# Another order of work at the border between two mixture-of-experts layers

## The chip, the core and the metric

The kernel runs as one launch on one of the eight cores of a Trainium2 chip. Its engines are TensorE (PE, matmuls and transposes; PEld is its weight load), VectorE (DVE), ScalarE (ACT), GpSimd (POOL) and SyncE (SP, which issues most DMAs); each runs its own queue of instructions in order. The metric is the device time of an execution in microseconds, the median of several runs.

## What is computed

A linear attention, then a mixture of experts with one expert for each token, then one with two experts for each token, all in float32:

```python
def reference(**kwargs):
    attn_out = _attn_ref(**attn_kwargs)      # state = alpha*state + k v^T; y = q state   (2 x 8 heads, 768 steps, 48)
    x = attn_out.transpose(0, 2, 1, 3).reshape(B * S, H * D)           # 1536 tokens x 384
    x = _moe_ref(x=x, **moe_kwargs)          # top 1 of 8: gate * (relu(x w1[e]) w2[e]), 384 -> 1024 -> 384
    return _moe2_ref(x=x, **moe2_kwargs)     # noisy top 2 of 8: sum of weight * (relu(x w1[e]) w2[e])
```

In the second layer a token's rows go to two experts, and the two weighted results are added in the output.

## The kernel before, in words

After the attention the kernel works through sixteen jobs, `n` = 0 to 15: the eight experts of layer 1, then the eight of layer 2. A job has a hidden product in eight blocks `f` (`hidden(n, f)`, L623, nine matmuls for each: every float32 product is made of three with operands split in two halves) and a second product in eight blocks (`second(n, f)`, L650, nine matmuls each). The weights come as raw tiles from DRAM (`raw(n, i)`, i = 0, 1 for the two halves of w1 at L505, 2, 3 for those of w2 at L508, 768 KB each, issued by SP). They are split into a high part by ACT (L523) and a low part by DVE or POOL (L524), a piece in each block. The rows of the next job are loaded with `load_x` (L566), transposed by PE and split by ACT and DVE (`split_x`, L582 to L587).

The order is written out by hand. Beside its own work a job advances the remains of the job before it, a generator `prev`: for layer 1 `job_route2` (the routing of the expert's results for layer 2, ending in four indirect DMAs that scatter rows into the DRAM store `xs2`, L158), for layer 2 `finish2` (results transposed by row tile at L834, weighted at L802 or L804, and added into `out` by an indirect DMA, L158). `STEPS` says how many steps `prev` takes in each of the sixteen blocks; one step is always taken ahead of the first block.

The change is at `n == E` (job 8), the first expert of layer 2. While it runs, the last job of layer 1 is still being routed. The rows that the last two experts of layer 1 send to expert 0 of layer 2 can't be there in time; they go into 128 rows of their own at `C0`, and are done apart. In block 3 of job 8's second product `load_late` asks SP for them (L841), and the generator `late_tokens` computes them: step 1 transposes them and splits them (L849 to L852), steps 2 and 3 make the hidden rows, nine matmuls of 512 columns each (L861), then the hidden rows are transposed (L874 to L877), and the last step makes the second product (L886) and adds it to `out`. Ahead of that, in block 0, `order` (L475 to L493) ranks the experts by their counts, so that from expert 2 on SP has to read the expert's number into a register before it can load its weights. The string `AFTER` is the order behind job 8's last block: `f` is a step of `finish2(8)`, `l` a step of `late_tokens`, `x` one of the three parts of `split_x` for expert 1.

PSUM banks are taken in turn from three pools: `pm` of two banks, `ph` of three, `py` of three. A tile waits until the one that had its bank before has been read.

Of the kernel before, what the change touches and what calls it, by code (L numbers as in the profile page):

```python
# [7 lines left out]
F32R = mybir.dt.float32r  # L8
# [8 lines left out]
N, DM, E, F = B * S, H * D, 8, 1024  # L17
# [8 lines left out]
CL = 128  # L26
# [29 lines left out]
LX = 9  # L56
SP = 7
WG = 8
STEPS = ("0110311010110000", "1311101110000000", "1021112010100000")
ENGS = ("VGGGGGGGGVVVVVGV", "GGGGGGGGGGGVGGVG")  # L60
XS = ("467", "267", "677")
LATE_F = 3
AFTER = "ffllxxllllxl"
SAFE = 1e-18
LOW1, LOW2, LOW3 = C1 - 128, C2 - 128, C2 - 256

# [1 line left out]
def body(tc, ap, cap, dbg=False, stop=False):  # L68
    nc = tc.nc
    V, A, G, PE = nc.vector, nc.scalar, nc.gpsimd, nc.tensor  # L70
    with ExitStack() as ctx:
# [15 lines left out]
        def hb(shape, dt=F32):  # L87
            return sb(shape, "h", 18, dt)
# [17 lines left out]
        def pm():  # L106
            return ps("pm", 2)
# [72 lines left out]
        ident = iw2[:, 0, :128]  # L180
# [315 lines left out]
        def raw(n, i):  # L496
            if n >= len(jobs):
                return
            layer = jobs[n][0]
            e = expert(n, mybir.EngineType.SP)  # L500
            one = slice(e, e + 1) if place(n) is None else bass.ds(e, 1)
            w1, w2 = ap[f"w1_{layer}"][one], ap[f"w2_{layer}"][one]
            if i < 2:
                t = s6([128, ND, 512])
                nc.sync.dma_start(t, w1.rearrange("o (d p) f -> p (o d) f", p=128)[:, :, i * 512:(i + 1) * 512])  # L505
            else:
                t = s6([128, 4, DM])
                nc.sync.dma_start(t, w2.rearrange("o (f p) d -> p (o f) d", p=128)[:, (i - 2) * 4:(i - 1) * 4, :])  # L508
            raws[n, i] = t
# [25 lines left out]
        def w2_of(n, f):  # L535
            hi, lo = parts[n, 2 + f // 4]
            return hi[:, f % 4, :], lo[:, f % 4, :]
# [19 lines left out]
        def load_x(n, eng):  # L557
            layer, e = jobs[n]
            nt_, p, c = dims(n)
            store = (xs1, xs2)[layer - 1]  # L560
            g = sb([p, nt_, RW], "b6", 5)
            if place(n) is None:
                rows_ = store[e * R:e * R + nt_ * p]
            else:
                rows_ = store[bass.ds(expert(n, eng.engine) * R, nt_ * p), :]
            eng.dma_start(g, rows_.rearrange("(t p) d -> p t d", p=p))  # L566
            xg[n] = g
            xsp[n] = (xb([128, ND, c], F32R), xb([128, ND, c], F32R))
# [275 lines left out]
        def late_tokens(n, g):  # L844

            xh, xl = xb([128, ND, CL], F32R), xb([128, ND, CL], F32R)
            xp = pm()
            for d in range(ND):
                PE.transpose(xp[:, d * CL:(d + 1) * CL], g[:, 0, d * 128:(d + 1) * 128], ident[:CL, :CL])  # L849
            m = lambda x: x.rearrange("p d c -> p (d c)")  # L850
            A.activation(m(xh), xp[:, :ND * CL], AF.Copy)
            V.tensor_tensor(m(xl), xp[:, :ND * CL], m(xh).bitcast(F32), op=ALU.subtract)  # L852
            yield
            hq = []
            for i in range(2):
                wh, wl = parts[n, i]
                p = ph()[:CL]
                for k in range(3 * ND):
                    d = k // 3
                    x, w = ((xh, wh), (xh, wl), (xl, wh))[k % 3]  # L860
                    PE.matmul(p, x[:, d, :], w[:, d, :], start=(k == 0), stop=(k == 3 * ND - 1))  # L861
                for q in range(2):
                    h = hb([CL, 256])
                    if q:
                        V.tensor_scalar(h, p[:, q * 256:q * 256 + 256], 0.0, None, op0=ALU.max)
                    else:
                        A.activation(h, p[:, :256], AF.Relu)
                    hq.append(h)
                yield
            ht = []  # L870
            for i in range(4):
                tp = pm()[:, :2 * CL]
                for k in range(2):
                    PE.transpose(tp[:, k * CL:(k + 1) * CL], hq[i][:, k * 128:k * 128 + 128], ident[:CL, :CL])  # L874
                hh, hl = hb([128, 2 * CL], F32R), hb([128, 2 * CL], F32R)
                A.activation(hh, tp, AF.Copy)
                V.tensor_tensor(hl, tp, hh.bitcast(F32), op=ALU.subtract)  # L877
                ht.append((hh, hl))
                if i % 2:
                    yield  # L880
            y = py()[:CL, :DM]
            for f in range(NF):
                (hh, hl), (wh, wl) = ht[f // 2], w2_of(n, f)
                sl = slice(f % 2 * CL, f % 2 * CL + CL)
                for k, (l, r) in enumerate(((hh, wh), (hh, wl), (hl, wh))):
                    PE.matmul(y, l[:, sl], r, start=(f == 0 and k == 0), stop=(f == NF - 1 and k == 2))  # L886
            ysc = hb([CL, 1, DM])
            weigh(g[:, :, NZ:NZ + 1], 0, y, tokens_of(g), ysc, [])
            yield
# [215 lines left out]
        for n, (layer, e) in enumerate(jobs):  # L1105
            steps = STEPS[0 if n < E else 1 if n == E else 2]
            eng = [G if x == "G" else V for x in ENGS[layer - 1]]
            step(prev)
            for f in range(NF):
                hidden(n, f)  # L1110
                split_rest()
                step(prev, int(steps[f]))
                if f == (3 if n == E - 1 else 0) and n not in (E, 2 * E - 1):
                    load_x(n + 1, nc.gpsimd)
                if f == 4 and layer == 2:
                    own_weight(n)
                if f % 4 == 2:
                    raw(n + 1, 2 + f // 4)
                if n != E + 1:
                    split(n + 1, f, eng[f])  # L1120
                else:
                    split(n, 8 + f, eng[f])
                    if f >= 4:
                        split_rest()
                        split(n + 1, f - 4, eng[f])
            if n < 2 * E - 1:
                for f in range(NF):
                    if n == E and f == LATE_F:
                        for _ in prev:
                            pass  # L1130
                        g = load_late(nc.sync)
                        load_x(n + 1, nc.sync)
                        it = late_tokens(n, g)
                    xs_ = XS[2 if n == 0 else layer - 1]
                    if n != E and str(f) in xs_:
                        split_x(n + 1, xs_.index(str(f)))
                    second(n, f, by_row(n))
                    split_rest()
                    step(prev, int(steps[8 + f]))
                    if n == E and f == 0:  # L1140
                        order(2, acc2)
                    if f % 4 == 2:
                        raw(n + 2, f // 4)
                    if n < 4 and f == 5:
                        zero_out(n)
                    if n != E:
                        split(n + 1, 8 + f, eng[8 + f])
                    if n == E + 1 and f < 4:
                        split_rest()
                        split(n + 1, 4 + f, eng[8 + f])  # L1150
                if n == E - NL:

                    cp = pm()
                    PE.matmul(cp[:, 0:1], ones, acc2[:, 0:1], start=True, stop=True)
                    V.tensor_scalar(eb3[:, 0:1], cp[:, 0:1], -1.0, float(C0), op0=ALU.mult, op1=ALU.add)
                    V.tensor_scalar(eb3[:, 0:1], eb3[:, 0:1], 0.0, None, op0=ALU.max)
                prev = job_route2(n) if layer == 1 else finish2(n)
                d = 0
                for o in AFTER if n == E else ():
                    if o == "x":  # L1160
                        split_x(n + 1, d)
                        d += 1
                    else:
                        step(prev if o == "f" else it)
            else:
                nt_, p, c = dims(n)
                ix = tokens_of(xg[n])
                ysc = sb([p, nt_, DM], "b6", 5)
                group = []
                it = beyond()  # L1170
                for t in range(nt_):
                    if t:
                        step(it)
                    for f in range(NF):
                        second(n, f, (t,))
                    weigh(own[n], t, yps[n][t][:tiles(n)[t][2], :DM], ix, ysc, group)
# [216 lines left out]
```

## Time and profile before

| | |
|---|---|
| runs, median (lowest to highest) | 500.62 us (499.69 to 501.07) |
| the profiled execution | 503.19 us, span 501.4 us |
| mean granted TensorE clock | 0.985 |
| PE busy | 478.2 us (95%), 3539 instructions |
| PEld busy | 448.2 us (89%) |
| DVE busy | 310.1 us (62%) |
| ACT busy | 262.0 us (52%) |
| POOL busy | 316.5 us (63%) |
| chain that ended last | PE 73%, DVE 14%, issue 4%, ACT 4%, DMA 2% |

The profile is of one execution; its times are counted from the start of its span. In the page's 40 slices of 12.5 us PE is at 9 tenths or more nearly throughout. Near the middle stands one slice at 7, the one from 275.8 to 288.3, and there alone the granted clock is below 9 tenths ahead of the last slice. This is where job 8 ends and job 9 begins: job 8's second product runs from 263.5 to 273.9, and the first hidden block of job 9 starts at 291.4. An engine's idle time costs nothing unless PE waits for it.

### The profile page before, as it was taken

The page shows a single profiled execution, that of the slowest core. Times are in us where ns is not written, and L with a number is a line of the kernel's source. Part 1 is how long each engine was busy: PE and PEld are TensorE (multiplying, and loading weights), DVE is VectorE, ACT ScalarE, POOL GpSimd, SP SyncE. Part 2 cuts the span into 40 slices and gives each one's busy share as a digit, 9 for nine tenths or more (in the row PEclk, how much of TensorE's full clock was granted, in tenths as well). Part 3 has the DMA queues.
Part 4 walks back from the last instruction along what each step waited for, and adds up shares of the span by engine and source line. Part 5 has one row for each costly group of instructions (what it writes and reads, how often), then busy time and mean ns, then how long its engine had stood idle before and what let it go on. Part 6 is the DMA issues. An engine that isn't in the chain of part 4 may idle for free.

```text
span 501.4 us, 9823 instructions
## 1 busy us (share of the span) xinstructions
PE 478.2 (95%) x3539; PEld 448.2 (89%) x3542; DVE 310.1 (62%) x866; ACT 262.0 (52%) x682; POOL 316.5 (63%) x396
## 2 busy tenths in 40 slices
PE   8997999899999999999999799999999999999993
PEld 4586887799999999999988699899999999999993
DVE  8999956656786786776863323925545373655540
ACT  3475686366675676675661248353554535364410
POOL 3444674374876786785864149697594958779322
PEclk9999998999999999999999899999999999999997
DMA  8974663497888777676734644393564927372132
GB/s 287 406 246 160 242 221 127 164 295 233 282 288 249 261 241 241 202 244 203 239 100 130 204 92 132 99 245 106 156 176 129 221 81 203 83 191 25 17 47 43
DMA packets 47798, 91.67 MB, mean 183 GB/s; under 512 B 4624, under 2 KB 29153, under 8 KB 47738
## 3 DMA queue, kind: packets, MB, share of 16 engines
q1 hardware_dynamic: 38090, 70.32, 42.9%
q0 software_dynamic: 9648, 20.61, 17.4%
q8 instruction: 30, 0.49, 0.4%
q14 instruction: 30, 0.25, 0.2%
HBM read 70.63 MB, written 20.28 MB: 181 GB/s over the span
## 4 chain that ended last, share of the span: by engine, by line
PE 73%; DVE 14%; issue 4%; ACT 4%; DMA 2%; POOL 1%; SPq 0%; POOLq 0%; DVEq 0%; ACTq 0%
PE py L650 28%; PE ph L623 27%; DVE s L524 2%; PE pm L582 2%; PE ph L290 2%; DVE h L627 2%; PE pm L366 2%; DVE s L237 2%; PE pm L834 1%; PE py L337 1%; PE pm L678 1%; PE py L343 1%; PE ph L861 1%; ACT s L523 1%; PE py L317 1%
## 5 line engine op out<-in xcount | busy, mean ns | idle before, releaser
L524 POOL TENSOR_TENSOR s<-s,s 128x384 fp32r<-128x384 f32 x175 | 184.8, 1301 | 51.0 <-ACT s L523 45.9
L623 PE MATMUL ph<-x,s 128*128 128x240 f32 (+6 forms) x1152 | 179.9, 311 | 3.1 <-DVE h L627 1.4
L623 PEld LDWEIGHTS ph<-x,s 128*128 128x128 f32 x1152 | 167.6, 189 | 6.9 <-DVE h L627 3.0
L650 PE MATMUL py<-h,s 128*128 128x240 f32 (+5 forms) x1008 | 154.1, 307 | 0.0
L650 PEld LDWEIGHTS py<-h,s 128*128 128x128 f32 x1008 | 142.5, 189 | 1.0
L523 ACT ACTIVATE s<-s 128x384 fp32r<-128x384 f32 x256 | 123.1, 516 | 0.0
L627 DVE SCALAR_TENSOR_TENSOR h<-ph,h 128x240 fp32r<-128x240 f32 (+6 forms) x128 | 61.0, 483 | 67.4 <-ACT h L626 62.0
L524 DVE TENSOR_TENSOR s<-s,s 128x384 fp32r<-128x384 f32 x81 | 89.8, 1128 | 5.6 <-ACT s L523 5.5
L626 ACT ACTIVATE h<-ph 128x240 fp32r<-128x240 f32 (+6 forms) x128 | 55.3, 432 | 62.8 <-PE ph L623 53.5
L158 POOL DMA_INDIRECT out<-b,m_ix x29 | 46.5, 1605 | 45.5 <-ACT b L802 21.0
L586 ACT ACTIVATE x<-pm 128x480 fp32r<-128x480 f32 (+7 forms) x38 | 18.5, 489 | 63.9 <-PE pm L582 63.5
L299 POOL TENSOR_SCALAR_AFFINE_SELECT h<-h 128x512 f32<-128x512 f32 x24 | 22.6, 964 | 39.2 <-ACT h L298 39.2
L158 POOL DMA_INDIRECT xs<-b,m_si x32 | 32.9, 1028 | 15.8 <-DVE pm L759 10.5
L587 DVE TENSOR_TENSOR x<-pm,x 128x480 fp32r<-128x480 f32 (+7 forms) x38 | 20.7, 550 | 31.8 <-ACT x L586 31.5
L650 PE MATMUL py<-s,h 128*128 128x384 f32 x144 | 26.6, 340 | 0.0
L650 PEld LDWEIGHTS py<-s,h 128*128 128x128 f32 x144 | 25.0, 188 | 0.0
L237 DVE TENSOR_TENSOR s<-s,s 112x256 f32<-112x256 f32 (+2 forms) x24 | 19.0, 813 | 0.8 <-DMA s<-qs 0.2
L158 POOL DMA_INDIRECT xs<-s,m_si x12 | 13.1, 1088 | 9.8 <-DVE m_g L405 4.6
L156 POOL MEMSET spacer<- 1x1 f32 x74 | 18.8, 253 | 0.1
L582 PE MATMUL pm<-iw,b 108*128 108x108 f32 (+5 forms) x129 | 18.5, 259 | 0.2 <-DVE accs L760 0.2
L170 PE MATMUL ph<-warm 128*128 128x512 bf16 x63 | 16.2, 410 | 1.7 <-POOL warm L165 1.5
L797 DVE TENSOR_REDUCE m_own<-m_ox 108x4 f32<-108x24 f32 (+1 forms) x6 | 1.1, 176 | 24.6 <-POOL m_ox L795 23.5
(234 smaller groups left out, 544.9 us busy)
## 6 DMA issues: line engine op xcount, KB each, us to landing
s<-w SPq DMA_DIRECT2D x64, 768.0 KB, 5.4
xs<-s SPq DMA_DIRECT2D x2, 1576.0 KB, 6.4
out<-s SPq DMA_DIRECT2D x4, 768.0 KB, 7.8
b<-xs POOLq DMA_DIRECT2D x4, 664.9 KB
b<-xs POOLq DMA_DIRECT2D x7, 369.4 KB
s<-as SPq DMA_DIRECT2D x2, 780.5 KB
s<-ks SPq DMA_DIRECT2D x2, 768.0 KB, 9.5
s<-qs SPq DMA_DIRECT2D x2, 768.0 KB
```

The source lines that it names most:

```text
L156: G.memset(spacer, 0.0)
L158: st = G.indirect_dma_start(out=dst, out_offset=bass.IndirectOffsetOnAxis(ap=ix, axis=0), in_=src, in_offset=None, **kw)
L237: eng.tensor_tensor(o, src[:, h].rearrange("r (s j) -> r s j", j=64), x[:, h].rearrange("r (s j) -> r s j", j=64), op=ALU.mult)
L299: G.affine_select(a_, a_, pattern=[[0, 4], [1, 128]], compare_op=ALU.is_ge, fill=0.0, base=0, channel_multiplier=-1)
L523: A.activation(hi[sl], t[sl], AF.Copy)
L524: rest.append(lambda: (eng or V).tensor_tensor(lo[sl], t[sl], hi[sl].bitcast(F32), op=ALU.subtract))
L582: PE.transpose(xp[:, k * c + sl.start:k * c + sl.stop], g[:r, t, d * 128:(d + 1) * 128], ident[:r, :r])
L587: V.tensor_tensor(m(xl), xp[:, :w], m(xh).bitcast(F32), op=ALU.subtract)
L623: PE.matmul(p, w, x[:, d, :], start=(k == 0), stop=(k == 3 * ND - 1))
L626: A.activation(hh, p, AF.Relu)
L627: V.scalar_tensor_tensor(hl, p, 0.0, hh.bitcast(F32), op0=ALU.max, op1=ALU.subtract)
L650: PE.matmul(out_, l, r, start=(f == 0 and k == 0), stop=(f == NF - 1 and k == 2))
```

## The change

Four things are altered. `STEPS` for job 8: the step that computes the row weights is taken in hidden block 5 and no longer in 6, and the rank matmul and the scatters follow together in hidden block 7, where the scatters before came in block 0 of the second product. The order behind job 8 (`AFTER`): the late rows are transposed ahead of row tile 0, row tile 1 comes ahead of the late products, and the transposes of the hidden rows alternate with those of expert 1's rows. The hidden rows of the late tokens are transposed four to a bank instead of two, the second four in a bank of `ph`, and evicted with half as many instructions of double width. And the load of the first half of w1 for job 10 stands on SP's queue behind the late rows' load and that of expert 1's rows, and no longer a block ahead of them.

```diff
-STEPS = ("0110311010110000", "1311101110000000", "1021112010100000")
+STEPS = ("0110311010110000", "1311110200000000", "1021112010100000")
-AFTER = "ffllxxllllxl"
+AFTER = "flfflllxlxxl"
@@ late_tokens
             ht = []
-            for i in range(4):
-                tp = pm()[:, :2 * CL]
-                for k in range(2):
-                    PE.transpose(tp[:, k * CL:(k + 1) * CL], hq[i][:, k * 128:k * 128 + 128], ident[:CL, :CL])
-                hh, hl = hb([128, 2 * CL], F32R), hb([128, 2 * CL], F32R)
+            for i in range(2):
+                tp = (pm, ph)[i]()[:, :4 * CL]
+                for k in range(4):
+                    PE.transpose(tp[:, k * CL:(k + 1) * CL], hq[2 * i + k // 2][:, k % 2 * 128:k % 2 * 128 + 128],
+                                 ident[:CL, :CL])
+                hh, hl = hb([128, 4 * CL], F32R), hb([128, 4 * CL], F32R)
                 A.activation(hh, tp, AF.Copy)
                 V.tensor_tensor(hl, tp, hh.bitcast(F32), op=ALU.subtract)
                 ht.append((hh, hl))
-                if i % 2:
-                    yield
+                yield
             y = py()[:CL, :DM]
             for f in range(NF):
-                (hh, hl), (wh, wl) = ht[f // 2], w2_of(n, f)
-                sl = slice(f % 2 * CL, f % 2 * CL + CL)
+                (hh, hl), (wh, wl) = ht[f // 4], w2_of(n, f)
+                sl = slice(f % 4 * CL, f % 4 * CL + CL)
@@ the second product's blocks
                         g = load_late(nc.sync)
                         load_x(n + 1, nc.sync)
+                        raw(n + 2, 0)
                         it = late_tokens(n, g)
...
-                    if f % 4 == 2:
+                    if f % 4 == 2 and (n, f) != (E, 2):
                         raw(n + 2, f // 4)
```

## Rows read from the trace of the kernel before

**Rows 1.** Chain of waits, 261 to 306: start, length, engine, tile, line, count.

```profile
265.19 8.42 PE py L650 x60
...
274.40 2.46 DMA h<-xs
...
278.03 3.84 PE ph L861 x9
...
282.61 2.12 PE ph L861 x9
...
291.31 0.33 PE pm L834 x3
...
293.75 12.37 PE ph L623 x63
```

**Rows 2.** Timeline of PE: start, length, instruction, idle before and releaser.

```profile
263.25 0.17 PE L743 MATMUL pm<-accs,tri 120*120 120x8 bf16 x1 [0.47 <-DVE m_wt L738]
...
276.90 0.55 PE L849 MATMUL pm<-iw,h 128*128 128x128 f32 x3 [2.06 <-DMA h<-xs]
...
285.98 0.77 PE L874 MATMUL pm<-iw,h 128*128 128x128 f32 x4 [0.83 <-DVE h L877]
...
323.25 1.25 PE L623 MATMUL ph<-x,s 128*128 128x432 f32 x5 [1.07 <-DVE x L587]
```

**Rows 3.** Timeline of SP's queue: end of layer 1, and the border.

```profile
100.17 0.37 SPq L606 DMA_DIRECT2D b<-xs  x1
...
268.47 0.00 SPq L505 DMA_DIRECT2D s<-w  x1
274.40 0.34 SPq L841 DMA_DIRECT2D h<-xs  x1
```

**Rows 4.** Waits of SP's queue, 240 to 345: total, times, longest.

```profile
SPq L841 <- DMA xs<-b,m_si: 5.9, 1, 5.9
```

**Rows 5.** Timeline of POOL: the last scatter of layer 1, and the border.

```profile
97.47 0.98 POOL L158 DMA_INDIRECT xs<-s,m_si  x1 [1.85 <-DVE acc L441]
...
257.95 6.84 POOL L524 TENSOR_TENSOR s<-s,s 128x384 fp32r<-128x384 f32 x7 [2.39 <-ACT s L523]
...
264.99 1.00 POOL L158 DMA_INDIRECT xs<-b,m_si  x1 [0.18 <-DVE accs L760]
...
268.89 0.99 POOL L158 DMA_INDIRECT xs<-b,m_si  x1 [0.22 <-issue]
...
291.84 1.61 POOL L158 DMA_INDIRECT out<-h,m_ix  x1 [14.43 <-ACT h L802]
...
296.96 1.60 POOL L158 DMA_INDIRECT out<-b,m_ix  x1 [3.47 <-DVE h L627]
...
300.78 21.00 POOL L524 TENSOR_TENSOR s<-s,s 128x384 fp32r<-128x384 f32 x21
```

**Rows 6.** Windows: PE, PEld, DVE, ACT, POOL busy; PEclk; DMA share; GB/s.

```profile
81.80:83.10 1.30, 0.06 (x2) 0.03 (x1) 0.68 (x2) 1.30 (x5) 0.00 (x0) 1.00 0.20 62
83.40:86.40 3.00, 3.00 (x16) 2.91 (x14) 2.00 (x8) 2.34 (x7) 1.25 (x3) 0.50 0.57 152
...
268.50:270.50 2.00, 2.00 (x16) 2.00 (x16) 0.00 (x0) 0.00 (x0) 1.24 (x4) 1.00 0.67 60
270.50:274.00 3.50, 3.50 (x27) 3.34 (x25) 0.37 (x1) 0.42 (x1) 0.00 (x0) 1.00 0.81 309
...
278.00:281.00 3.00, 2.97 (x7) 2.40 (x8) 0.56 (x1) 0.00 (x0) 0.00 (x0) 0.50 0.93 286
```

**Rows 7.** Timeline of ACT and DVE: the late rows' copies, one subtraction, a split.

```profile
277.48 0.49 ACT L851 ACTIVATE x<-pm 128x384 fp32r<-128x384 f32 x1 [2.02 <-PE pm L849]
278.00 0.56 DVE L852 TENSOR_TENSOR x<-pm,x 128x384 fp32r<-128x384 f32 x1 [3.23 <-ACT x L851]
...
311.91 10.30 DVE L524 TENSOR_TENSOR s<-s,s 128x384 fp32r<-128x384 f32 x1 [0.69 <-ACT s L523]
...
320.07 0.52 ACT L523 ACTIVATE s<-s 128x384 fp32r<-128x384 f32 x1
```

## The prediction

> **What bounds the kernel now.** I read the page first: TensorE (PE) is busy 95% of the span, no other engine above 63%, so only what stands on PE's way can move the end. The 40 slices show one place in the middle where PE falls to 7 and its clock to 8: the border between the two layers. Then I read the chain of waits there [rows 1], PE's own idle times [rows 2], and what SP and POOL were doing [rows 3 to 5]. The reader is to see this. PE works without a gap from 265.19 for 8.42 us, to 273.61, on expert 0's second product. It then transposes row tile 0 and stands for 2.06 us, until the late rows arrive [rows 2]. They were asked for at 274.40, since SP stood 5.9 us at that load for the scatters that write those rows [rows 3, 4]. The first product on the late rows then runs at half speed: nine matmuls take 3.84 us, the next nine 2.12 [rows 1], and the granted clock is 0.50, the 1.2 GHz level [rows 6]. A last gap of 0.83 us follows at the transposes of the late hidden rows [rows 2]. Far behind, at 323.25, PE waits 1.07 us for a piece of x of expert 2 [rows 2].
>
> The sum is made in the profiled execution: 501.4 us of span, 503.19 us in all. The median of the runs is 500.62, 2.57 lower; I take the difference in time over to the median unchanged.
>
> **The change, part by part.** Times at which nothing is said of a source are those of the step before plus the named duration.
>
> Row weights a block ahead. In the trace PE waits 0.47 us at L743 for the row weights' product (DVE L738) [rows 2], though the rank matmul doesn't use it; it shares its PSUM bank. One hidden block earlier that product is done before PE asks. The 0.47 us is not won: the next thing PE needs is the count in the matmul of `order` (L475), whose operand DVE writes last of all (L760, just before the first scatter [rows 5]). PE reaches that matmul earlier and waits there. DVE's chain itself only moves by the order of a tenth, since its last links hang on the last hidden block's eviction. Cost and gain: 0 (bounds: 0.47 gained, 0.2 lost by a later sixth eviction, which nobody waits for).
>
> The scatters. They are now emitted ahead of the last of the seven POOL subtractions (6.84 us for seven [rows 5], 0.98 each). POOL is free 0.98 us earlier, but the row numbers come from DVE, so the first scatter can gain between 0 and 0.98; I take 0.25, since DVE's L760 ended only 0.18 us before it started. The last then ends its issue at 268.89 + 0.99 - 0.25 = 269.63.
>
> The weight load behind the late rows' load. This is the largest term. Before, SP issued 768 KB of weights at 268.47, in the middle of the four scatters, and was released by the scatters at 274.40, that is 4.52 us after the last scatter's issue ended [rows 3, 5]. The weight load is in flight for just this time: from 268.5 to 270.5 the transfers move 60 GB/s with the engines two thirds busy, and only then does the rate rise [rows 6]. The nearest row without such a neighbour is the last scatter of layer 1: issued at 97.47 for 0.98 us, SP released at 100.17, 1.72 us after [rows 3, 5]. So the landing takes between 1.72 and 4.52 us; I take 1.72, for the same kind of transfer with nothing beside it. SP then issues the late rows' load at 271.35, and at 2.46 us [rows 1] plus 0.04 they are there at 273.85. Upper end: 274.15 and 276.65.
>
> A page speaks against this. The Trainium skill, "DMA: Bandwidth & Descriptors", section "Anatomy of one DMA — SWDGE (gpsimd) path", puts about 2.0 us of a transfer down to a fixed cost, mostly the receipt of the last write, heaviest for DRAM; no removal of traffic shortens that. With about half a microsecond of data it would make some 2.5 us (an estimate from that page) where the row has 1.72, and the sum some 0.8 us smaller; 1.72 measured here already includes such a receipt, so the row decides.
>
> What the moved weight load costs: SP's register load, the load of expert 1's rows and then the weights follow at about 272.5 instead of 268.47. The weights are split first in the fourth block of expert 1's hidden layer, near 300; a load of that size lands in single microseconds. Cost 0. Behind the waiting late load on SP stand expert 1's rows and two weight loads; the rows go out about 3 us earlier than before, so nobody waits longer for them.
>
> Late transposes ahead of the row tiles. PE finishes the second product at 273.61 and finds the late rows at 273.85: a wait of 0.24 us in place of 2.06. Row tile 0 moves behind them, into the time in which ACT and DVE copy the transposed rows (ACT starts 0.58 us after PE, 0.49; DVE ends 1.66 us after PE's start [rows 2, 7]). But tile 1 is now third in a pool of two banks and waits for DVE's copy: to 273.85 + 1.66 = 275.51. With its 0.33 us [rows 1] the first late product starts at 275.85; before it was 278.03. Gain 2.18.
>
> From there to the second hidden block of expert 1 the trace has 293.75 - 278.03 = 15.72 us [rows 1]. Off this go: 3.84 - 2.12 = 1.72, if the clock stays at its upper level, because the wait before is 0.24 + 0.8 and not 2.06; the 0.83 us gap, now filled by a group of expert 1's transposes; and 0.33 for tile 1, already counted. Rest 12.84.
>
> Four to a bank. Eight transposes stay eight; four pairs of evictions become two pairs of double width. Nothing at 512 columns of this kind stands in the trace: between the 384-column rows of 0.49 (ACT) and 0.56 (DVE) [rows 7] and a third more, 0.65 and 0.75. The new order puts the second and third x groups behind these copies on DVE, each in a bank that must be free; I work out waits on PE of about 0.5 and 0.25 us. So plus 0.75 (0 to 1.6). 12.84 + 0.75 = 13.59, and the second hidden block starts at 275.85 + 13.59 = 289.44. Border gain: 293.75 - 289.44 = 4.31 us.
>
> The wait at 323. One DVE subtraction, two operands in SBUF, took 10.30 us from 311.91 [rows 7], until POOL's run of 21 subtractions, 21.00 us from 300.78 [rows 5], was over; the split of x behind it made PE wait 1.07 us. POOL started that run late: tile 1's scatter stood from 293.5 to 296.96 behind the late rows' scatter of 291.84, then came tile 2's and a load [rows 5]. With tile 1's scatter moved ahead of the late one, one step of 1.91 us falls out. Against PE's second hidden block, the run began 300.78 - 293.75 = 7.03 us after it. Now the late product ends 2.11 us before that block (2.44 from tile 1 to it [rows 1], less one tile), its scatter follows 0.9 later, the run 8.94 - 1.91 = 7.03 us after that: 5.82. POOL is 1.21 us ahead and through with twenty of the 21 at 319.57 on the old scale; the operand of the last comes at 320.59 [rows 7], so POOL pauses a microsecond and DVE gets through: 1.07 us gained. It needs a lead of more than 0.2 us. The Trainium skill, "SBUF — State Buffer", section "SBUF: two separate sides", says that a DVE instruction with two SBUF inputs and a GpSimd one exclude each other for a whole instruction; by that rule alone DVE would wait for one subtraction, about 1 us, and the wait at 323 would not hang on POOL's start. The row has 10.30, so the trace decides.
>
> Sum: 4.31 + 1.07 = 5.38. The profiled execution would take 503.19 - 5.38 = 497.8, the median 500.62 - 5.38 = 495.24, so 495.2.
>
> **The rivals.**
> (a) The clock falls again: PE's small waits (0.24, then 0.8 with a few transposes between) are enough. For it: a wait of 1.24 us (1.30 with 0.06 of work) was followed by 0.50 from 83.40 on [rows 6]. Against: the 1.07 us at 322 had no such effect (the page's clock row stays at 9). Price 1.72: 3.66 gained, 497.0.
> (b) The wait at 323 stays, because POOL's lead is eaten on its way: 4.31, 496.3. With (a) as well: 2.6, 498.0.
> (c) The scatters land no faster without the weight load, at 276.65 the late rows come as before, and PE, which can no longer do tile 0 first, stands 3 us. The first late product starts at 276.65 + 1.66 + 0.33 = 278.64, at half speed: 278.64 + 13.59 + 1.72 = 293.95, 0.2 later than before, against 1.07 won: 499.8. For it: the four scatters are 480 separate rows and not 128. Against: their bytes flow at POOL's pace until the weights come in.
> (d) Slower: as (c), but PE stays at the low level through both late products and into the third. A low stretch costs half its length. Without it (c) would gain 293.75 - 292.23 + 1.07 = 2.59, so it decides from 5.2 us at the low level; the stretches in the trace lasted a little over 3 us [rows 6]. Three of them at 3.3, 9.9 us, cost 4.95 and give 500.62 + 2.36 = 503.0.
>
> **How the numbers follow.** Forecast 0.46, with its own range of 494.4 to 496.4 (the two bounds of the x waits and 0.7 us of landing); (a) 0.16; (b) 0.14; (a) with (b) 0.05; (c) 0.15; (d) 0.04. About 0.3%, 1.5 us, is what a measurement can tell. Faster: the first four and a little of (c), 0.82; same 0.13; slower 0.05. The range runs from 494.0 to 499.0: it takes in (a), (b) and both, leaves out (c) and (d).
>
> **What would show it.** The late load's issue near 271.4 and under 2 us behind the last scatter; no weight load in flight then; PE's wait at L849 under 0.5 us, a new one of about 0.8 at L834, none of 0.83 at L874; both groups of nine at L861 near 2.1 us; the clock row without the 8; a new wait of about 0.4 at L475; two evictions of 128x512; tile 1's scatter ahead of the late one; no DVE subtraction of 10 us and no wait of 1.07 at L623. The prediction is wrong if the late load is still issued near 274, or if L861's first nine still take 3.8.

## The result and the profile after

The changed kernel takes 494.86 us, median of four runs (494.43 to 495.22), where the kernel before took 500.53 beside it (499.69 to 501.07): a ratio of 0.9888, 95% interval 0.9871 to 0.9905, so 5.67 us less. 495.2 was forecast. The later groups of runs were on chips on which the kernel before takes between 501.5 and 505.0 us, so there only ratios are compared.

The two profiled executions differ by 8.8 us, more than the medians. Job 8 already starts 2.47 us earlier (247.81 against 250.28), ahead of anything that was changed. Another 0.69 us lies in job 8's hidden blocks, where the execution before has a wait of 0.56 us for DVE. That wait comes and goes whatever the kernel: the changed kernel's second profile has it (0.57), and before_fill, with the old `STEPS`, has it not. So I compare distances between three marks on PE that lie behind it: R, the long run of job 8's second product behind `order`; H, the first hidden block of expert 1; K, expert 2's hidden blocks behind its first row tile. PE's timeline of the kernel before (start, length, instruction) has them here:

```profile
265.05 8.96 PE L650 MATMUL py<-h,s 128*128 128x304 f32 x63
...
291.40 2.02 PE L623 MATMUL ph<-x,s 128*128 128x432 f32 x9
...
293.50 12.61 PE L623 MATMUL ph<-x,s 128*128 128x432 f32 x63
...
321.23 0.95 PE L623 MATMUL ph<-x,s 128*128 128x432 f32 x4
...
324.34 0.83 PE L834 MATMUL pm<-iw,b 128*108 128x128 f32 x3
324.93 3.79 PE L623 MATMUL ph<-x,s 128*128 128x432 f32 x18
```

And PE's timeline of the changed kernel, with the idle time before an instruction and its releaser in brackets:

```profile
261.85 0.18 PE L475 MATMUL pm<-accs,ones 128*128 128x8 bf16 x1 [0.58 <-DVE accs L760]
261.89 8.97 PE L650 MATMUL py<-h,s 128*128 128x304 f32 x63
271.03 0.52 PE L849 MATMUL pm<-iw,h 128*128 128x128 f32 x3 [0.17 <-DMA h<-xs]
...
272.60 0.54 PE L834 MATMUL pm<-iw,b 128*108 128x128 f32 x3 [0.73 <-ACT b L802]
272.89 4.41 PE L861 MATMUL ph<-s,x 128*128 128x512 f32 x18
277.13 0.60 PE L874 MATMUL pm<-iw,h 128*128 128x128 f32 x4
...
279.15 1.10 PE L582 MATMUL pm<-iw,b 108*128 108x108 f32 x8 [0.48 <-DVE h L878]
...
284.29 0.49 PE L834 MATMUL pm<-iw,b 128*88 128x128 f32 x3
284.54 14.39 PE L623 MATMUL ph<-x,s 128*128 128x432 f32 x72
...
314.05 1.94 PE L623 MATMUL ph<-x,s 128*128 128x432 f32 x9
315.83 0.49 PE L834 MATMUL pm<-iw,b 128*108 128x128 f32 x3
316.07 3.79 PE L623 MATMUL ph<-x,s 128*128 128x432 f32 x18
```

R to H was 26.35 and is 22.65; H to K was 33.53 and is 31.53; together 59.88 and 54.18, that is 5.70 less, as much as the 5.67 of the medians. The reader is to see four things. The wait for the late rows is 0.17 us and no longer 2.06 [rows 2]. All eighteen matmuls on the late rows take 4.41 us, where the first nine alone took 3.84 [rows 1]. The 0.83 ahead of L874 has gone, and three waits are new: 0.58 at L475, 0.73 at row tile 1, 0.48 at the x groups. And nothing waits at 314, where 1.07 stood [rows 2].

SP's queue shows why the late rows are there:

```profile
268.51 0.34 SPq L841 DMA_DIRECT2D h<-xs  x1
269.07 0.33 SPq L566 DMA_DIRECT2D b<-xs  x1
270.27 1.13 SPq L505 DMA_DIRECT2D s<-w  x2
```

And POOL's timeline shows the last scatter, then the late rows' scatter, tile 2's, and the run of subtractions:

```profile
265.55 0.98 POOL L158 DMA_INDIRECT xs<-b,m_si  x1 [0.22 <-issue]
...
285.40 1.59 POOL L158 DMA_INDIRECT out<-h,m_ix  x1 [8.95 <-ACT h L802]
290.46 1.60 POOL L158 DMA_INDIRECT out<-b,m_ix  x1 [3.43 <-DVE h L627]
...
293.00 19.50 POOL L524 TENSOR_TENSOR s<-s,s 128x384 fp32r<-128x384 f32 x20
313.48 1.01 POOL L524 TENSOR_TENSOR s<-s,s 128x384 fp32r<-128x384 f32 x1 [0.97 <-ACT s L523]
```

The late load goes out 268.51 - 266.53 = 1.98 us behind the end of the last scatter's issue, where it was 4.52 [rows 3, 5]. The DMA queues show what was in the way. POOL's scatters go through the queue q0, SP's loads through q1; each row has packets, MB, and share of the 16 DMA engines. This is all that moved in the kernel before from 268.90 to 271.50, that is 3.85 to 6.45 us behind R, with the scatters still to land:

```profile
q1 hardware_dynamic: 192, 0.39, 81.5%
```

And in the changed kernel the same distance behind R, from 265.74 to 268.34:

```profile
q0 software_dynamic: 128, 0.38, 53.1%
```

While the weights come in, the scatters' queue stands still for 2.6 us, about the 2.54 by which they land later (4.52 - 1.98). Why it stands still no run here shows.

POOL's run has a pause of 0.97 us ahead of its last subtraction, and there DVE gets through; on DVE's timeline the two subtractions end at 313.40, ahead of PE's need:

```profile
278.40 0.69 DVE L878 TENSOR_TENSOR h<-pm,h 128x512 fp32r<-128x512 f32 x1 [0.23 <-ACT h L877]
...
304.73 8.67 DVE L524 TENSOR_TENSOR s<-s,s 128x384 fp32r<-128x384 f32 x2 [0.69 <-POOL s L524]
```

### The profile page after: what moved, and what is told of

Same layout as the page of the kernel before. It is cut to its first block, busy times and chain, and to the rows that moved or that the text cites. A ratio compares the mean times of both kernels' runs of the same rounds, so it can differ in the third digit from the quotient of the medians.

```text
span 492.7 us, 9819 instructions
## 1 busy us (share of the span) xinstructions
PE 475.2 (96%) x3539; PEld 446.8 (91%) x3542; DVE 315.1 (64%) x864; ACT 262.0 (53%) x680; POOL 315.8 (64%) x396
## 4 chain that ended last, share of the span: by engine, by line
PE 80%; DVE 11%; ACT 3%; issue 3%; DMA 2%; POOL 1%; SPq 0%; POOLq 0%; DVEq 0%
PE py L650 31%; PE ph L623 30%; PE pm L582 3%; PE ph L290 2%; PE pm L366 2%; PE py L337 2%; DVE s L237 2%; PE pm L834 2%; DVE h L627 1%; DVE s L524 1%; PE py L343 1%; PE pm L678 1%; PE py L317 1%; PE py L284 1%; DVE s L254 1%
## 5 line engine op out<-in xcount | busy, mean ns | idle before, releaser
L524 DVE TENSOR_TENSOR s<-s,s 128x384 fp32r<-128x384 f32 x81 | 95.2, 1195 | 4.4 <-ACT s L523 3.6
L299 POOL TENSOR_SCALAR_AFFINE_SELECT h<-h 128x512 f32<-128x512 f32 x24 | 21.6, 921 | 39.4 <-ACT h L298 39.4
```

The lines of the kernel that those rows point to most:

```text
L299: G.affine_select(a_, a_, pattern=[[0, 4], [1, 128]], compare_op=ALU.is_ge, fill=0.0, base=0, channel_multiplier=-1)
L524: rest.append(lambda: (eng or V).tensor_tensor(lo[sl], t[sl], hi[sl].bitcast(F32), op=ALU.subtract))
```

## The experiments

The theory: the weight load beside the scatters delayed their landing, the wait for the late rows let the clock fall, and the new order starts POOL's run early enough for DVE. The rival: the order of work carries the gain, and the load was hidden anyway. The marks of all kernels, each from one profiled execution, in us:

| kernel | R to H | H to K | sum | ratio to before, 95% interval |
|---|---|---|---|---|
| before | 26.35 | 33.53 | 59.88 | |
| changed | 22.65 | 31.53 | 54.18 | 0.9888 (0.9871 to 0.9905) |
| changed, second group | 22.70 | 31.54 | 54.24 | 0.9865 (0.9836 to 0.9895) |
| changed, third group | 22.74 | 31.53 | 54.27 | 0.9863 (0.9835 to 0.9892) |
| load_only | 22.85 | 33.38 | 56.23 | 0.9910 (0.9877 to 0.9943) |
| no_load_move | 26.70 | 31.53 | 58.23 | 0.9971 (0.9939 to 1.0004) |
| no_steps | 22.98 | 31.53 | 54.51 | 0.9878 (0.9814 to 0.9942) |
| decoy | 29.33 | 31.53 | 60.86 | 1.0017 (0.9988 to 1.0047) |
| before_fill | 25.13 | 33.52 | 58.65 | 0.9974 (0.9949 to 1.0000) |
| tile1_late | 22.25 | 33.99 | 56.24 | 0.9927 (0.9898 to 0.9955) |
| two_to_bank | 26.05 | 31.50 | 57.55 | 0.9940 (0.9914 to 0.9966) |
| tile1_between | 22.44 | 31.53 | 53.97 | 0.9876 (0.9846 to 0.9907) |
| tile1_between_ph | 22.55 | 31.53 | 54.08 | 0.9864 (0.9835 to 0.9892) |
| best | 22.64 | 31.42 | 54.06 | 0.9850 (0.9823 to 0.9878) |

Where row tile 2 comes behind expert 1's first block (before, load_only, before_fill, tile1_late), it takes 0.33 us of H to K (two blocks start 2.10 us apart with it between them, 1.77 without); elsewhere it takes 0.25 of R to H (284.54 - 284.29). The three profiles of the changed kernel agree within 0.09 us. The runs alone set load_only apart from the kernel before; the intervals of no_load_move, before_fill and decoy reach 1, so what is said of these three rests on the traces.

**load_only**: one edit on the kernel before.

```diff
                         load_x(n + 1, nc.sync)
+                        raw(n + 2, 0)
...
-                    if f % 4 == 2:
+                    if f % 4 == 2 and (n, f) != (E, 2):
```

> The kernel before with the weight load of expert 2 moved behind the late rows' load, and nothing else. Theory (traffic and clock): without the load beside them the scatters land about 2 us after the last issue instead of 4.5, the late load goes out 2.5 us earlier, PE's wait at the late transposes shrinks from 2.06 to under 0.5 us, and with it the half-speed stretch of the first late product goes (1.7 us). The gap of 0.83 at the hidden rows' transposes and the wait at 323 stay. About 3.7 us faster, 496.8. Rival (the order of work is what counts, the load is hidden anyway): less than 1.5 us, 499 or more.

PE's timeline, with SP and POOL under it:

```profile
276.80 0.49 PE L849 MATMUL pm<-iw,h 128*128 128x128 f32 x3
278.01 2.48 PE L861 MATMUL ph<-s,x 128*128 128x512 f32 x9 [0.72 <-ACT x L851]
...
321.70 1.24 PE L623 MATMUL ph<-x,s 128*128 128x432 f32 x5 [0.89 <-DVE x L587]
```

```profile
273.95 0.34 SPq L841 DMA_DIRECT2D h<-xs  x1
```

```profile
270.97 0.98 POOL L158 DMA_INDIRECT xs<-b,m_si  x1 [0.21 <-issue]
```

3.65 us less between the marks, where 3.7 were expected; the landing is 273.95 - 271.95 = 2.00 us, PE doesn't wait at L849, and the wait far behind stays. The first nine matmuls take 2.48 us for 3.84, which is 1.36 of the 1.7 expected there. This edit alone is two thirds of the gain; the rival falls.

**no_load_move**: the changed kernel without that edit.

> The changed kernel with the weight load back at its old place ahead of the late load; row weights, order and banks as changed. Theory: the scatters land 4.5 us after their issue again, the late rows come near 276.5 on the old scale, PE stands some 3 us and the first late product runs at 1.2 GHz; only the wait at 323 and the gap of 0.83 are won: 498.3 to 499.7. Rival (order counts, load is hidden): within 0.7 us of the changed kernel, 495.5.

PE's timeline, SP's queue, and windows (PE, PEld, DVE, ACT, POOL busy; PEclk; DMA share; GB/s):

```profile
277.48 0.52 PE L849 MATMUL pm<-iw,h 128*128 128x128 f32 x3 [2.91 <-DMA h<-xs]
...
279.59 5.48 PE L861 MATMUL ph<-s,x 128*128 128x512 f32 x18
```

```profile
274.88 0.34 SPq L841 DMA_DIRECT2D h<-xs  x1
```

```profile
278.00:282.00 4.00, 3.28 (x12) 2.55 (x11) 1.18 (x2) 0.96 (x2) 2.44 (x3) 0.57 0.98 323
```

The late load goes out 4.62 us behind the last scatter's issue (270.26), PE stands 2.91 us, the clock falls to 0.57, and R to H is even 0.35 longer than before. The border is then about what rival (c) of the prediction has (0.2 later), though (c) has the scatters land late without the weight load too, and load_only shows that they don't. The 1.65 us that are left come from behind H, where 2.00 are won.

**decoy**: a copy at the old place, for nobody.

```diff
+        decoy = dram.tile([DM, F], F32, name="decoy")
...
+                    if (n, f) == (E, 2):
+                        nc.sync.dma_start(decoy, ap["w1_2"][bass.ds(expert(n + 2, mybir.EngineType.SP), 1)].rearrange("o d f -> (o d) f"))
```

> The changed kernel with one DMA more: the same 768 KB of expert 2's weights copied from DRAM to a DRAM scratch, issued by SP where the weight load stood before; nobody reads it. Theory (bytes in flight delay the scatters): the landing goes back from 2.0 to 4 us or more, the late load goes out 2 to 3 us later, PE's wait at the late transposes is 2 to 3 us, the clock falls behind it: 498 to 500. Rival (it is not the bytes but what the weight load did to buffers or to SP's order): as the changed kernel, 494.9 within 0.5.

From the copy's buffer on this kernel's line numbers are higher by one, so L842 here is L841 in the others. SP's queue, its issue of the copy with the size, POOL's last scatter, and PE:

```profile
276.60 0.35 SPq L842 DMA_DIRECT2D h<-xs  x1
```

```profile
decoy<-w SPq DMA_DIRECT2D x1, 1536.0 KB
```

```profile
269.60 0.99 POOL L159 DMA_INDIRECT xs<-b,m_si  x1 [0.22 <-issue]
```

```profile
279.16 0.87 PE L850 MATMUL pm<-iw,h 128*128 128x128 f32 x3 [4.28 <-DMA h<-xs]
```

The last scatter's issue ended at 270.59, so the landing took 6.01 us, and PE stood 4.28. The copy was to be of the weight load's size, but it takes all of expert 2's w1, 1536 KB where the load has 768, and it writes them to DRAM too. 498 to 500 was expected, and the marks put it 0.98 us above the kernel before, so I had its price about 1.5 us or more too low. So it is no measure of the weight load's own price. What it shows is that a transfer that nobody reads, and that has none of the weight load's buffers, delays the scatters as well: from 271.05 to 274.75 only q1 has packets. It stands on SP's queue where the load stood, so by itself it doesn't rule out SP's order; but in both kernels SP did nothing behind that issue but wait for the scatters (5.9 us [rows 4] and 7.2).

**before_fill**: the kernel before, with useless matmuls in the wait.

```diff
-AFTER = "ffllxxllllxl"
+AFTER = "ffwllxxllllxl"
...
+                    elif o == "w":
+                        warm(9)
```

> The kernel before with nine matmuls of 128x512 on a constant tile put on PE between row tile 0 and the late rows' transposes, nothing else: work that nobody uses, in the wait of 2.06 us. Theory (the wait lets the granted clock fall, and that is what the first late product pays): the clock stays at 2.4 GHz, the first nine matmuls take 2.1 to 2.5 us and not 3.84, the late rows come as before: 1.2 to 1.8 us faster than the kernel before. Rival (the product is slow because of the transfers beside it, or its operands come late): 3.8 us still, no difference.

```profile
272.03 1.89 PE L170 MATMUL ph<-warm 128*128 128x512 bf16 x8
274.10 0.55 PE L849 MATMUL pm<-iw,h 128*128 128x128 f32 x3 [0.18 <-DMA h<-xs]
275.23 2.48 PE L861 MATMUL ph<-s,x 128*128 128x512 f32 x9 [0.58 <-ACT x L851]
```

```profile
276.00:278.00 2.00, 2.00 (x11) 1.48 (x12) 0.00 (x0) 0.26 (x1) 0.00 (x0) 1.00 0.86 291
```

Eight of the nine are recorded. The late rows come no earlier (their transposes start 11.92 us behind R, before 11.85), yet the first nine matmuls take 2.48 us at a granted clock of 1.00, with 291 GB/s of transfers beside them: 1.23 us less in all. The wait set the clock, not the transfers.

**no_steps**: the old `STEPS` string in the changed kernel.

> The changed kernel with the old STEPS string (row weights and scatters a block later). Theory: the wait of 0.47 at the rank matmul comes back, the new wait of 0.58 at the matmul of the counts goes, the scatters start 0.3 us later, and PE waits 0.3 us more for the late rows: 0 to 0.5 us slower than the changed kernel, 494.9 to 495.4. Rival (the earlier scatters carry the gain): 1.5 us or more slower, 496.4 and up.

Behind R it is 0.24 to 0.33 us longer; PE waits 0.50 for the late rows. Ahead of R the 0.47 and the 0.58 trade places: from PE's readiness for the rank matmul to R it is 262.78 to 265.05, 2.27 us, before [rows 2], and 259.51 to 261.89, 2.38 us, changed. From job 8's start to R the old string takes 14.77 to 14.79 us in the profiles that have the wait of 0.56 for DVE, and the new one 14.71 to 14.76. The runs can't tell this from nothing.

**tile1_late**: row tile 1 goes back into expert 1's job.

```diff
-AFTER = "flfflllxlxxl"
+AFTER = "flflllxlxxl"
```

> The changed kernel with row tile 1 not ahead of the late products but in expert 1's job, as before (one step fewer behind job 8). Theory (POOL's lead ends the wait far behind): PE has no wait of 0.73 for tile 1's bank and starts the late product 0.7 us earlier, but tile 1's scatter stands behind the late one again, POOL's run of subtractions starts 1.9 us later, the DVE subtraction takes 10 us again and PE loses 1.1 us at expert 2's first hidden block and about 0.6 at the row tile behind it: 0.5 to 1.3 us slower than the changed kernel. Rival (the wait at 323 went for another reason, such as the earlier border): 0.7 us faster than the changed kernel.

```profile
319.13 1.25 PE L623 MATMUL ph<-x,s 128*128 128x432 f32 x5 [1.55 <-DVE x L587]
```

```profile
296.66 21.00 POOL L524 TENSOR_TENSOR s<-s,s 128x384 fp32r<-128x384 f32 x21
```

POOL's run has no pause again and PE waits 1.55 us. The direction was right, the size was not: 2.0 us slower than the changed kernel between the marks, not 0.5 to 1.3. PE gained 0.4 at the border and not 0.7, and 0.25 of it is only tile 2, now behind H; there 2.46 were lost, 0.33 of them by tile 2. POOL's run starts 7.74 us behind expert 1's second block (296.66 - 288.92), later than in the kernel before (300.78 - 293.50 = 7.28), and so the wait is longer than 1.07.

**two_to_bank**: the changed kernel with the four banks of two from before (the lines that follow from this are left out).

```diff
-            for i in range(2):
-                tp = (pm, ph)[i]()[:, :4 * CL]
+            for i in range(4):
+                tp = pm()[:, :2 * CL]
```

> The changed kernel with the hidden transposes two to a bank again, all in the pool of two. Theory: with the x groups between them the two banks turn over more often, each turn waiting for a copy on ACT and DVE: 0.5 to 1.5 us more between the late product and expert 1's first block. Rival (the width of the evictions doesn't matter, or shorter ones free the banks sooner): within 0.3 us of the changed kernel, or faster.

```profile
278.06 0.59 PE L582 MATMUL pm<-iw,b 108*128 108x108 f32 x4 [0.82 <-DVE h L877]
...
281.96 5.41 PE L886 MATMUL py<-s,h 128*128 128x384 f32 x24
```

```profile
277.00:279.00 2.00, 1.05 (x9) 0.57 (x7) 1.09 (x3) 1.08 (x4) 0.00 (x0) 1.00 1.10 322
279.00:281.00 2.00, 0.94 (x6) 0.59 (x6) 1.13 (x3) 0.99 (x4) 0.00 (x0) 0.92 1.07 284
281.00:283.00 2.00, 1.71 (x7) 1.71 (x8) 0.97 (x3) 0.96 (x2) 0.00 (x0) 0.50 0.43 146
```

3.3 us more, where I expected 0.5 to 1.5. PE is busy half of the time from 277 to 281 in short waits for copies, and then the clock falls as it did behind a long wait; the late rows' second product takes 5.41 us for 4.43. I had left that out.

**tile1_between**, **tile1_between_ph**, **best**: attempts to take the new waits away.

```diff
-AFTER = "flfflllxlxxl"
+AFTER = "flflfllxlxxl"        # tile1_between, tile1_between_ph
+AFTER = "flflfllxlfxxl"       # best
...
-                tp = (pm, ph)[i]()[:, :4 * CL]
+                tp = ph()[:, :4 * CL]        # tile1_between_ph, best
```

> The changed kernel with row tile 1 between the two late products (order f l f l f l l x l x x l). Theory: its bank is free by then, so the wait of 0.73 on PE goes, and its scatter is still ahead of the late one: 0.5 to 0.8 us faster than the changed kernel. Rival (the wait only moves to the expert's transposes, whose banks hang on the same DVE copies): within 0.2 us of it.

> The kernel with tile 1 between the late products, and both banks of hidden transposes taken from the pool of three. Theory: the wait of 0.48 at the second x group goes, since its bank no longer hangs on the copy of the first four; the third group still waits for DVE, some 0.25 us: 0.2 to 0.5 us faster than with tile 1 between alone. Rival (DVE's copies are the bound, whatever the bank): within 0.1 us of it.

> Tile 1 between the late products, both banks of hidden transposes from the pool of three, and row tile 2 also behind job 8, ahead of the second x group (order f l f l f l l x l f x x l). Theory: tile 2's transposes fill half of the wait of 0.62 at the x groups, tile 1's wait of 0.73 stays away, and POOL, which no longer has to wait for the late scatter's landing, starts its run some 5 us earlier: 0.4 to 0.8 us less than the changed kernel in the trace, hardly to be told in the runs. Rival (DVE's copies bound the stretch whatever PE does between): within 0.2 us in the trace.

The changed kernel ran beside them twice:

> The changed kernel once more, as the measure for the three beside it: 1.0 to 1.3% faster than the kernel before (5.2 to 6.3 us).

> The changed kernel again, as the measure for the others of this group: 1.0 to 1.4% faster than the kernel before, 54.2 us from the second product's long run to expert 2's second hidden block.

The second group's 0.9865 is 1.35% less time, slightly more than the 1.0 to 1.3% expected; the third's 0.9863, 1.37%, is inside its range. tile1_between was to gain 0.5 to 0.8 and missed that: the late product starts 1.09 us behind L849 and not 1.86; half a microsecond of that goes back, since tile 1's transposes now part the two groups, and 0.2 to 0.3 are left. With both banks from the pool of three the wait of 0.48 goes, and one of 0.62 stands at the third x group, now for DVE's copy of the first: nothing is gained, the rival's case. In the last one tile 2's transposes fill it in part, and the late scatter has nothing queued behind it; POOL then runs in pieces and DVE's two subtractions end sooner:

```profile
294.98 15.63 POOL L524 TENSOR_TENSOR s<-s,s 128x384 fp32r<-128x384 f32 x16 [0.82 <-ACT s L523]
```

```profile
304.95 6.53 DVE L524 TENSOR_TENSOR s<-s,s 128x384 fp32r<-128x384 f32 x2 [0.69 <-ACT s L523]
```

PE needed none of that. The rival was right here too: 0.1 to 0.2 us. Its runs gave 494.22 us beside 495.04 for the changed kernel, 0.9850 against 0.9863 with intervals that overlap, so that it beats the changed kernel is not shown.

## Why the prediction was right

Row weights a block ahead: right, nothing gained. The 0.47 at the rank matmul went, and 0.58 came at the matmul of the counts, as said; from the rank matmul to R 0.11 worse, from job 8's start to R some 0.05 better.

The scatters: 0.25 expected; the first one stands 0.22 us ahead of R and stood 0.06 ahead, so 0.16.

The landing: right in mechanism, slightly too fast: 1.72 forecast, 1.98 measured, and 2.00 and 2.06 in load_only and no_steps. The page of the Trainium skill that spoke against it ("DMA: Bandwidth & Descriptors", "Anatomy of one DMA — SWDGE (gpsimd) path"), with the some 2.5 us estimated from its 2.0 of fixed cost, lies 0.5 us above the measured value, and the row of layer 1 lies 0.26 below it. The measurement decides. SP is released 0.44 us after the scatters' last packet (0.49 in the kernel before), so here a receipt of the last write is not most of the landing.

PE's wait for the late rows is 0.17, forecast 0.24, but that they agree is chance. The prediction lets PE end the second product at 273.61, the end of the 60 matmuls that the chain of waits names [rows 1]; all 63 end at 265.05 + 8.96 = 274.01. And the late rows' transposes start 9.14 us behind R (271.03 - 261.89), 0.34 later than forecast (273.85 - 265.05 = 8.80); 0.26 of that is the landing. The moved weights cost nothing, as forecast: PE has no wait for them between the marks.

Tile 1's bank: PE starts the late product 1.86 us behind L849 by its rows, and 2.11 by the chain of waits, from which the 2.00 were forecast. The profile puts the 0.73 of waiting down to ACT's weighing of tile 0, which ends at 272.54; DVE's copy that I had named ends at 272.67 by its row, 0.07 behind PE's start. That this copy was what PE waited for is not shown.

The clock: right. Eighteen matmuls in 4.41 us at a granted clock of 1.00 (271.0 to 277.3), and before_fill shows it by itself.

From the late product to H: forecast 13.59 less one block of 1.78, so 11.81; it is 11.65. The copies of 512 columns take 0.60 (ACT) and 0.69 us (DVE), estimated at 0.65 and 0.75. The first x wait is 0.48, worked out at 0.5; the second, 0.25, has no row of its own.

The wait at 323 is the term that was mis-sized: 1.07 forecast, 1.67 measured (2.00 from H to K less the 0.33 of tile 2). I took the one idle time that PE's rows name. In the same rows, the nine matmuls and what interrupts them take 1.33 us more than in the changed kernel (321.23 to 324.34, now 314.05 to 315.83), and row tile 0 behind them stood another 0.35 for its copy on DVE, which was late for the same reason. A mark on both sides would have shown the whole price. POOL's run began 7.03 us behind expert 1's second block (300.78 - 293.75), and in the changed kernel 6.45 behind it (that block is at 284.78 + 1.77 by the chain of waits, the run at 293.00): its lead is 0.58 and not the 1.21 worked out, since POOL took 2.54 us from tile 2's scatter to its run where 1.91 was counted. A shorter run, 19.50 us for twenty subtractions, made up for that, and what decides, the pause ahead of the last one, is 0.97 us long where one microsecond was forecast. DVE's subtraction still stands for 8.2 us there, where none of 10 was forecast; it ends in time.

Sum: 5.38 forecast; 5.70 between the marks, 5.67 in the medians. The border gave 4.03 (3.70 from R to H and the 0.33 of tile 2) for 4.31, the wait 1.67 for 1.07. The mechanisms are as forecast, but that the sum is right to 0.3 us is in part luck, since the two errors have opposite signs.

## What to carry to other kernels

A transfer that nobody waits for can still be paid for, by the one beside it that somebody waits for: look at what is in flight while a scatter or a small load on the critical chain lands, and move the bulk load behind it. A wait of PE can cost its own length and then the low clock behind it, so look for both: behind waits of 2.06 and 2.91 us at this border the granted clock fell, behind 1.07 and 1.55 far from it the clock stayed at 1.00; many short waits for copies did the same as one long one. And where an engine waits far behind a border, follow the chain back through the helper's queue (here a scatter that stood on another scatter's landing, then POOL's run, then DVE), and price it between two marks, not by the one idle time that is named.

## What the runs showed that I had not expected

Four scatters land 2.0 to 2.2 us after their last issue by themselves, 4.5 to 4.7 beside a load of 768 KB, and 6.0 beside a DRAM copy of 1536 KB; beside either their queue moves no packet for some 2.5 us or more. One DVE subtraction of 0.55 us can stand for 10.30 us beside POOL's unbroken run, ten of POOL's instructions, and goes at POOL's first pause. DVE's evictions from PSUM aren't held up by the same run:

```profile
303.19 0.61 DVE L627 SCALAR_TENSOR_TENSOR h<-ph,h 128x432 fp32r<-128x432 f32 x1 [1.16 <-ACT h L626]
```

And in two_to_bank the granted clock fell to 0.50 though PE was busy for half of the time before.
